# DeltaNet recurrence and MLP mixer in fp32: all four batch elements walk their Grams, joins and recurrence in 64 and 32 wide tiles

## The chip, the cores and the metric

One core of a Trainium2 chip. The kernel is one program for five engines: TensorE (PE, with its weight loads as PEld), VectorE (DVE), ScalarE (ACT), GpSimd (POOL) and SyncE (SP), each of which runs its own instructions in order and waits on semaphores for the others. The metric is the device time of one execution in microseconds (us), lower is better. Everything is fp32.

## The reference

Two parts. The first is a delta rule recurrence, for each of 4 batch elements and 8 heads, over 768 tokens of 48 features:

```python
k_n = k / (np.linalg.norm(k, axis=-1, keepdims=True) + 1e-06)
state = np.zeros((B, H, D, D), dtype=np.float32)
for t in range(S):
    kt, vt, bt = (k_n[:, :, t], v[:, :, t], beta[:, :, t, None])
    y[:, :, t] = np.einsum('bhd,bhde->bhe', q[:, :, t], state)
    v_old = np.einsum('bhde,bhd->bhe', state, kt)
    state = state + bt[:, :, :, None] * np.einsum('bhd,bhe->bhde', kt, vt - v_old)
```

The second takes y as x of shape (4, 768, 384), the heads side by side, and mixes it over tokens and then over channels:

```python
xt = x.transpose(0, 2, 1)
h = np.maximum(xt @ w_tok1, 0.0) @ w_tok2
u = x + h.transpose(0, 2, 1)
h2 = np.maximum(u @ w_ch1, 0.0) @ w_ch2
return (u + h2).astype(np.float32)
```

The weights arrive as float64 and are turned into fp32 on the chip.

## The kernel before

A **unit** u is 128 tokens of one batch element, 24 in all, six to an element. It has two **chunks** of 64 tokens (cc = 0, 1). A **step** t is one chunk of the recurrence, 48 in all, twelve to an element. The 8 heads are taken as 4 pairs p, so a unit has 8 blocks nb = 2p + cc, each for a pair of heads. With a head's 64 rows on half of the 128 partitions, a pair fills them.

The work is split into jobs, Python generators that issue a few instructions between two `yield`s. One letter and one number name a job: `k` loads k and q, `v` loads v, `p` prepares a unit, `i` inverts the triangular blocks of a round of units, `h`, `f` and `j` join the inverted blocks, `r` is a step of the recurrence, `m` is the mixer of an element, `w` turns a piece of weights into fp32. Three more, `x`, `y` and `z`, only multiply zeros on PE and write a PSUM tile that nobody reads. A long string, `order`, written out by hand, says which job moves on next, word by word, and so sets the order of the instructions on every engine. Nothing else schedules.

What a unit goes through:

- `prep` (`p`): k and q are transposed on PE (p_t), ACT copies them to kqt, with features on partitions and tokens along the free side. Then the Gram p_g, k times [k|q], is made for every block, and DVE multiplies it by the mask and by beta into gm. In the first element (u < NCH = 6) it is made per head, with 64 wide weights, one head on each half (line 387). In the other three, ACT first copies k into kbd, a tile of 128x128 blocks with one head in each diagonal corner and zeros elsewhere (line 360), and one 128 wide matmul makes the block of a pair (line 385).
- `invert` (`i`): DVE inverts 32x32 triangular blocks for a whole round of units at once, 14 or 30 pairs of instructions (lines 507 and 512). From the second element on, the blocks pass through DRAM (n_dram, w_dram).
- `join` (`j`): two 32x32 inverses are joined into one of 64x64 by two products p_z and p_x. The first element uses 32 wide tiles (lines 575 and 584), the others zero-padded tiles t11 and zst that make each product 65 columns wide over all 128 partitions (lines 604 and 613).
- `recur` (`r`): for a chunk, r = k·state - v, w = W·r with W the joined inverse, state and y from w. `recur_early` does the first element per head: p_k, p_y, p_w, p_s, and p_y again, 64 wide, head 0 from rows 0 to 63 to rows 0 to 63 and head 1 from rows 64 to 127 to rows 64 to 127. `recur` does the others on pairs: s_bd, r_bd and w_bd hold the two heads' tiles in two corners of a 128x96 block and zeros elsewhere. p_q (line 719) is k·state and q·state in one matmul for a pair, p_w (735) and p_s (743) follow. DVE writes r_bd in two halves (722), ACT copies the q half of p_q into the mixer's input xb (726) and w_bd in two halves (738), DVE updates s_bd (751) and adds the rest of y to xb (759).

`mixer` (`m`) is the same for all elements: p (line 772), p_h (785), then for six chunks of 128 tokens p_ut, p_c with a relu on ACT (811, 819) and p_o (827), which DVE adds to xb (833) and a DMA writes out. The steps of a later element stand between pieces of the mixer of the one before: m0 among units 6 to 17 or so, m1 and m2 after it, and m3 alone at the end.

PSUM has four kinds of buffer: prep (2), seq (2), mlp (3) and warm (1, for the zeros).

## Time and profile before

| | |
|---|---|
| median of 3 runs | 786.44 us (786.2 to 787.96) |
| the profiled execution's own time | 786.3 us |
| span of its trace, first to last instruction | 784.5 us |
| PE busy | 742.1 us, 95% of the span |
| DVE busy | 383.0 us, 49% |
| ACT busy | 256.0 us, 33% |
| POOL busy | 99.5 us, 13% |
| mean granted TensorE clock | 0.952 |

Times below are us from the start of the span. An fp32 matmul stands in the trace as two passes, each with its own weight load, so a count of passes is twice that of the matmuls. Passes overlap in the records: a pass of 128 columns is listed with some 0.28 us though the next may start 0.11 us after it. How long a group takes is therefore read from its start to the start of the next one. A busy share of 95% says that PE always had something in flight, not that it worked at its peak. The granted clock (PEclk) is 1 at full speed and 0.5 when it is halved.

### The profile page before, as it was taken

The page shows a single profiled execution, that of the slowest core. Times are in us where ns is not written, and L with a number is a line of the kernel's source. Part 1 is how long each engine was busy: PE and PEld are TensorE (multiplying, and loading weights), DVE is VectorE, ACT ScalarE, POOL GpSimd, SP SyncE. Part 2 cuts the span into 40 slices and gives each one's busy share as a digit, 9 for nine tenths or more (in the row PEclk, how much of TensorE's full clock was granted, in tenths as well). Part 3 has the DMA queues.
Part 4 walks back from the last instruction along what each step waited for, and adds up shares of the span by engine and source line. Part 5 has one row for each costly group of instructions (what it writes and reads, how often), then busy time and mean ns, then how long its engine had stood idle before and what let it go on. Part 6 is the DMA issues. An engine that isn't in the chain of part 4 may idle for free.

```text
span 784.5 us, 16847 instructions
## 1 busy us (share of the span) xinstructions
PE 742.1 (95%) x6950; PEld 607.9 (77%) x6950; DVE 383.0 (49%) x983; ACT 256.0 (33%) x589; POOL 99.5 (13%) x122
## 2 busy tenths in 40 slices
PE   8879987988899999997899999999999999999998
PEld 6558886657789789776588888778888978688776
DVE  6987778898735724337433538231228433200000
ACT  4546566427543113322124431233121322111110
POOL 2121234314320001110001010010000000000000
PEclk9976568799999999999799999999999999999999
DMA  7834345436524033232032231300011120000000
GB/s 152 170 84 98 84 104 136 92 99 152 132 55 103 14 84 64 36 72 44 13 79 42 47 64 24 83 21 12 21 29 23 35 42 1 11 11 11 11 11 21
DMA packets 151101, 46.82 MB, mean 60 GB/s; under 512 B 142416, under 2 KB 145488, under 8 KB 151024
## 3 DMA queue, kind: packets, MB, share of 16 engines
q1 hardware_dynamic: 151024, 45.74, 26.6%
q8 instruction: 55, 0.90, 0.5%
q14 instruction: 22, 0.18, 0.1%
HBM read 36.27 MB, written 9.44 MB: 58 GB/s over the span
## 4 chain that ended last, share of the span: by engine, by line
PE 79%; DVE 11%; SPq 3%; issue 2%; ACT 2%; DMA 2%; POOL 1%; POOLq 0%; ACTq 0%; DVEq 0%
PE p_o L827 24%; PE p_c L811 23%; PE p_g L385 4%; PE p_s L743 3%; PE p_q L719 3%; PE p L772 3%; DVE x L512 3%; PE p_w L735 3%; DVE sub L507 2%; SPq L292 2%; PE p_h L785 2%; PE p_z L604 2%; PE p_x L613 2%; PE p_t L353 1%; PE p_w L665 1%
## 5 line engine op out<-in xcount | busy, mean ns | idle before, releaser
L827 PE MATMUL p_o<-wc,r 128*128 128x384 f32 x576 | 199.2, 493 | 9.0 <-ACT r L819 8.3
L811 PE MATMUL p_c<-u_t,wc 128*128 128x128 f32 x1728 | 206.5, 276 | 0.6 <-ACT u_t L799 0.6
L811 PEld LDWEIGHTS p_c<-u_t,wc 128*128 128x128 f32 x1728 | 200.0, 192 | 5.1 <-ACT u_t L799 0.8
L827 PEld LDWEIGHTS p_o<-wc,r 128*128 128x128 f32 x576 | 106.3, 192 | 72.2 <-ACT r L819 8.5
L819 ACT ACTIVATE r<-p_c 128x512 f32<-128x512 f32 x72 | 42.9, 597 | 202.1 <-PE p_c L811 201.7
L833 DVE TENSOR_TENSOR xb<-xb,p_o 128x384 f32<-128x384 f32 x24 | 13.3, 554 | 152.6 <-PE p_o L827 152.6
L507 DVE TENSOR_TENSOR sub<-x 128x84 f32<-128x84 f32 (+24 forms) x178 | 61.7, 347 | 10.8 <-DMA x<-n_dram 6.0
L512 DVE TENSOR_TENSOR x<-x,sub 128x84 f32<-128x84 f32 (+24 forms) x178 | 63.3, 356 | 6.1
L364 POOL TENSOR_TENSOR mb<-mask_c,cs 128x512 f32<-128x512 f32 x20 | 21.6, 1079 | 253.2 <-DVE cs L343 217.0
L390 DVE TENSOR_TENSOR gm<-p_g,mb 128x512 f32<-128x512 f32 x48 | 32.7, 685 | 37.1 <-PE p_g L385 31.9
L751 DVE TENSOR_TENSOR s_bd<-s_bd,p_s 48x192 f32<-48x192 f32 x60 | 21.4, 357 | 56.5 <-PE p_s L743 55.3
L230 POOL TENSOR_TENSOR w_f<-w_f,d 128x384 uint32<-128x384 uint32 (+1 forms) x34 | 33.8, 996 | 112.8 <-DVE w_f L223 59.6
L726 ACT COPY xb<-p_q 64x384 f32<-64x384 f32 x33 | 15.7, 475 | 98.9 <-DVE r_bd L722 96.8
L385 PE MATMUL p_g<-kqt,kbd 128*128 128x128 f32 x288 | 41.4, 294 | 1.8 <-ACT kqt L373 0.7
L385 PEld LDWEIGHTS p_g<-kqt,kbd 128*128 128x128 f32 x288 | 38.0, 205 | 6.3 <-ACT kqt L373 1.8
L302 POOL TENSOR_TENSOR v_st<-v_st,nrm 128x384 f32<-128x384 f32 x24 | 20.2, 845 | 177.7 <-DMA v_st<-in_v_dram 167.5
L722 DVE TENSOR_TENSOR r_bd<-p_q,v_st 64x192 f32<-64x192 f32 x66 | 23.1, 350 | 32.9 <-PE p_q L719 18.5
L719 PEld LDWEIGHTS p_q<-s_bd,kqt 128*128 128x128 f32 x264 | 32.9, 192 | 5.3 <-issue 2.4
L772 PE MATMUL p<-xb,w 128*128 128x384 f32 x96 | 34.4, 491 | 1.8 <-DVE w L232 1.8
L719 PE MATMUL p_q<-s_bd,kqt 128*128 128x96 f32 x264 | 34.6, 274 | 1.1 <-DVE s_bd L751 1.1
L785 PE MATMUL p_h<-r,w 128*128 128x384 f32 x96 | 33.7, 492 | 2.0 <-DVE xb L789 1.9
L743 PEld LDWEIGHTS p_s<-w_bd,gm 128*112 128x112 f32 x288 | 32.1, 178 | 3.6 <-ACT w_bd L738 0.6
(122 smaller groups left out, 907.4 us busy)
## 6 DMA issues: line engine op xcount, KB each, us to landing
d<-in_moe_w_ch_dram SPq DMA_DIRECT2D x24, 384.0 KB, 3.4
kpad<-in_k_dram SPq DMA_DIRECT2D x24, 192.0 KB, 3.7
kst<-in_k_dram SPq DMA_DIRECT2D x96, 48.0 KB, 2.7
qpad<-in_q_dram SPq DMA_DIRECT2D x24, 192.0 KB, 3.6
v_st<-in_v_dram SPq DMA_DIRECT2D x96, 48.0 KB, 2.4
out_dram<-xb SPq DMA_DIRECT2D x24, 192.0 KB, 1.9
n_dram<-gm SPq DMA_DIRECT2D x72, 32.0 KB, 1.7
gm<-w_dram SPq DMA_DIRECT2D x72, 32.0 KB, 2.1
```

What stands on the lines that cost most here:

```text
L230: nc.gpsimd.tensor_tensor(out=f, in0=f, in1=lo, op=ALU.add)
L385: nc.tensor.matmul(p_g[:, i], kbd[:, nb], kqt[:, nb])
L390: nc.vector.tensor_tensor(out=gm[:, r, 0 : 2 * C].rearrange("s b (two n) -> s b two n", two=2), in0=p_g, in1=mb.rearrange("s p c t -> s (p ...
L507: nc.vector.tensor_tensor(out=tmp, in0=y[:, :, 0:s, s : s + 1].to_broadcast([n, k, s, w]), in1=y[:, :, s : s + 1, s + 1 : m].to_broadcast( ...
L512: nc.vector.tensor_tensor(out=y[:, :, 0:s, s + 1 : m], in0=y[:, :, 0:s, s + 1 : m], in1=tmp, op=ALU.add,)
L719: nc.tensor.matmul(p_q[:, p], kqt[:, 2 * p + cc], s0[:, p])
L743: nc.tensor.matmul(p_s[0 : C + D, p], gm[:, 2 * p + cc, C:], w_bd[:, p])
L772: nc.tensor.matmul(p_1[dh], piece_of(w1, c, 0)[:, dh * 128 : (dh + 1) * 128], xb[:, c], start=(c == 0), stop=(c == NCH - 1),)
L785: nc.tensor.matmul(p_h, piece_of(w2, j, c * 128)[:, c * 128 : (c + 1) * 128], r1[j], start=(j == 0), stop=(j == NDH - 1),)
L811: nc.tensor.matmul(p_c[:, i], piece_of(wc1, cb, f * 128)[:, f * 128 : (f + 1) * 128], u_t[:, cb], start=(cb == 0), stop=(cb == NCB - 1),)
L819: nc.scalar.activation(r, p_c, ACTF.Relu)
L827: nc.tensor.matmul(p_o, r2[f // FG][:, f % FG], piece_of(wc2, f, 0), start=(f == 0), stop=(f == NHT - 1),)
```

## The change

All four elements now go the way of the first one, per head, in 64 wide and 32 wide tiles:

- kbd, the zero-padded t11 and zst, and the block-diagonal r_bd, w_bd and s_bd are gone, with the copies and clears that they needed. `recur_early` becomes `recur`, and the two branches of `prep` and `join` become one.
- In odd chunks the two heads change places where tokens are on partitions: beta, k and v are loaded with `PAR[par ^ cc]`. A product from features to tokens of head i then goes from rows of half i to rows of half i ^ cc.
- In a Gram, p_g of chunk 0 uses the tiles (rows low, columns low) and (high, high), that of chunk 1 (low, high) and (high, low). The four are issued one after the other, for each pair, into two PSUM buffers. Both buffers are now taken at once.
- In a step, p_k and the first part of p_y are issued together, pair by pair: p_k goes to half i ^ cc and p_y to the other half, so that again four tiles are used in turn. p_s and the second part of p_y are issued together in the same way. p_y collects both parts in PSUM (in the buffer of the zeros from the second element on), and ACT writes it to xb in two halves at the end of the step. DVE's addition to xb and ACT's copy from p_q are gone.
- p_w, p_z and p_x keep two tiles side by side.
- The order string is new up to about step 15, with more words x, y and z (x 15 to 40, y 16 to 62, z 12 to 22). After that it is the old one, with one more word for each step and fewer for `prep`. A y is now half as long: 128 columns instead of 256.

PE's order at step 21 (second element; unit 10 in kqt_104 before and kqt_103 after). Before:

```order
L743 MATMUL p_s<-w_bd,gm 112x96 x4
L811 MATMUL p_c<-u_t,wc_130 128x128 x3
L385 MATMUL p_g<-kqt_103,kbd 128x128 x8
L811 MATMUL p_c<-u_t,wc_130 128x128 x6
L719 MATMUL p_q<-s_bd_117,kqt_104 128x96 x4
L811 MATMUL p_c<-u_t,wc_130 128x128 x6
L735 MATMUL p_w<-r_bd,gm 65x96 x4
```

And now (line 696 is the mixer's p_c, 603 and 604 are p_k and p_y, which go on alternating up to eight of each):

```order
L629 MATMUL p_s<-w_st_114,gm 48x48
L630 MATMUL p_yb<-w_st_114,gm 64x48
L696 MATMUL p_c<-u_t,wc_129 128x128 x3
L376 MATMUL p_g<-kqt_102 64x128 x16
L696 MATMUL p_c<-u_t,wc_129 128x128 x6
L603 MATMUL p_k<-s_st_117,kqt_103 64x48
L604 MATMUL p_yb<-s_st_117,kqt_103 64x48
```

The pieces of the mixer between the groups are the same; each group has two or four times as many matmuls as before.

ACT's order at step 26 (third element, unit 13), around the copy from p_q. Before:

```order
L327 ACTIVATE ksq<-kst 128x384
L799 COPY u_t<-p_ut 128x384
L819 ACTIVATE r_4243<-p_c 128x512
L619 COPY gm<-p_x 32x8x32 x2
L726 COPY xb<-p_q 64x384
L819 ACTIVATE r_4299<-p_c 128x512
L819 ACTIVATE r_4314<-p_c 128x512
L799 COPY u_t<-p_ut 128x384
```

And now (704 is the relu, 684 the copy of u_t, 576 that of p_x):

```order
L322 ACTIVATE ksq<-kst 128x384
L684 COPY u_t<-p_ut 128x384
L704 ACTIVATE r_5005<-p_c 128x512
L576 COPY gm<-p_x 32x8x32 x2
L704 ACTIVATE r_5059<-p_c 128x512
L704 ACTIVATE r_5074<-p_c 128x512
L684 COPY u_t<-p_ut 128x384
```

Nothing that belongs to step 26 stands between the relus any more.

PE's order in the first element, from step 0's p_s to step 1's p_w. Before:

```order
L675 MATMUL p_s<-w_bd,gm 48x48 x8
L688 MATMUL p_y<-w_bd,gm 64x48 x8
L552 MATMUL p_x<-gm,xb 16x16 x32
L575 MATMUL p_z<-t_112,gm 32x32 x16
L646 MATMUL p_k<-s_bd_117,kqt_100 64x48 x8
L656 MATMUL p_y<-s_bd_117,kqt_100 64x48 x8
L665 MATMUL p_w<-r_bd,gm 64x48 x8
```

And now, from the last pair of step 0 to the first of step 1 (line 376 is a Gram of unit 5, line 168 a word y, of four matmuls with zeros):

```order
L629 MATMUL p_s<-w_st_114,gm 48x48
L630 MATMUL p_y<-w_st_114,gm 64x48
L376 MATMUL p_g<-kqt_104 64x128 x16
L168 MATMUL p_warm_132<-warm 64x128
L168 MATMUL p_warm<-warm 64x128 x2
L168 MATMUL p_warm_132<-warm 64x128
L603 MATMUL p_k<-s_st_117,kqt_99 64x48
L604 MATMUL p_y<-s_st_117,kqt_99 64x48
```

A word y has come in ahead of step 1, and three more stand between its p_y and its p_w, where PE went from one straight to the other.

The core of the diff:

```diff
@@ warm_tiles
-                        (p_warm_2 if i == k else p_warm)[out_r, 0:2], warm[r, 0:C],
-                        warm[r, None, 0:128].to_broadcast([C, 2, 128]),
+                        (p_warm_2 if i == k else p_warm)[out_r, 0], warm[r, 0:C],
+                        warm[r, 0:128],
@@ stacked
-                    out=dst[C * par : C * par + C, :, cc], in_=rows[par, cc]
+                    out=dst[PAR[par ^ cc], :, cc], in_=rows[par, cc]
@@ prep
         nc.scalar.copy(kqt_k, p_t)
-        for par in range(2 if u >= NCH else 0):
-            nc.scalar.copy(bd[PAR[par], :, :, C * par : C * par + C], p_t[PAR[par]])
...
-                if u >= NCH:
-                    nc.tensor.matmul(p_g[:, i], kbd[:, nb], kqt[:, nb])
-                for r in PAR if u < NCH else ():
-                    nc.tensor.matmul(p_g[r, i], kqt[r, nb, 0], kqt[r, nb])
...
+        p_g = [ps_prep([128, NP, 2, C], "p_g") for cc in range(2)]
+        for p in range(NP):
+            for cc in range(2):
+                for i in range(2):
+                    nc.tensor.matmul(
+                        p_g[cc][PAR[i ^ cc], p], kqt[PAR[i], 2 * p + cc, 0],
+                        kqt[PAR[i], 2 * p + cc],
+                    )
@@ join, units 6 to 23
-            nc.tensor.matmul(p_z[0 : C + 1, nb], gm_of(u)[:, nb, 0 : C + 1], t11[:, nb])
+            for r, r2 in halves:
+                nc.tensor.matmul(p_z[r2, nb], wt[r, nb, HB:C], t11[r, nb])
...
+                nc.tensor.matmul(p_x[r, nb], zst[r2, nb], wt[r2, nb, HB:C])
@@ recur
-                nc.tensor.matmul(p_q[:, p], kqt[:, 2 * p + cc], s0[:, p])
...
-            nc.scalar.copy(y, p_q[hi].rearrange("s p n -> s (p n)"))
...
+        if b == 0:
+            p_y = ps_mlp([128, NP, D], "p_y")
+        else:
+            p_y = psum.tile([128, NP, D], FP32, name="p_yb", tag="warm", bufs=1)
...
+            for p, i in by_head:
+                f = FEATS[i]
+                nc.tensor.matmul(p_k[PAR[i ^ cc], p], kqt[f, 2 * p + cc, 0], s0[f, p])
+                nc.tensor.matmul(
+                    p_y[PAR[1 - (i ^ cc)], p], kqt[f, 2 * p + cc, 1], s0[f, p],
+                    start=(p == 0), stop=False,
+                )
+            yield
+            nc.vector.tensor_tensor(out=r_st, in0=p_k, in1=v_st[:, :, cc], op=ALU.subtract)
...
+        nc.scalar.copy(w, p_w)
...
+            r = PAR[i ^ cc]
+            if not last:
+                nc.tensor.matmul(p_s[FEATS[i], p], gm[r, 2 * p + cc, 2 * C :], w[r, p])
+            nc.tensor.matmul(
+                p_y[PAR[1 - (i ^ cc)], p], gm[r, 2 * p + cc, C : 2 * C], w[r, p],
+                start=(c == 0 and p == 0), stop=(p == NP - 1),
+            )
...
-        p_y = p_s[lo].rearrange("s p n -> s (p n)")
-        if c > 0:
-            nc.vector.tensor_tensor(out=y, in0=y, in1=p_y, op=ALU.add)
...
+        for i in range(2):
+            nc.scalar.mul(
+                y[:, :, D * i : D * i + D], p_y[PAR[1 - (i ^ cc)]], 1.0 if c else -1.0
+            )
@@ jobs
-        jobs[f"r{t}"] = recur(t) if t >= NQ else recur_early(t)
+        jobs[f"r{t}"] = recur(t)
```

336 lines of the change are left out of this document (105 added, 231 removed).

## The prediction

> **What bounds the kernel now.** I read the span and then a view that cuts it into stretches. The columns are the stretch, its length, the busy time and instructions of PE, PEld, DVE, ACT and POOL, the granted clock, and the DMA share and rate.
>
> ```profile
> span 784.5 us, 16847 instructions
> 0.00:216.20 216.20, 187.38 (x3054) 151.22 (x3055) 177.80 (x438) 115.67 (x269) 63.19 (x78) 0.85 0.53 119
> 50.00:100.00 50.00, 45.09 (x1116) 40.35 (x1116) 38.92 (x101) 30.41 (x76) 14.16 (x15) 0.66 0.43 93
> 100.00:150.00 50.00, 44.13 (x940) 38.63 (x941) 41.90 (x101) 29.13 (x72) 16.23 (x18) 0.73 0.51 114
> 216.20:668.40 452.20, 443.01 (x3248) 370.42 (x3247) 197.47 (x532) 125.40 (x292) 36.35 (x44) 0.99 0.21 43
> 668.40:784.50 116.10, 111.72 (x651) 86.27 (x649) 7.75 (x14) 14.92 (x29) 0.00 (x0) 1.00 0.04 13
> ```
>
> There are three stages. From 216 to 668 us PE is busy for 443.01 of 452.20 us and DVE for less than half: PE bounds, and nearly all that it lacks is one stop, below. From 668 us m3 runs alone, which the change does not touch. Up to 216 us DVE has 177.80 us of work and PE 187.38, at a clock that is halved for long (0.66 and 0.73 between 50 and 150 us): two engines that wait for each other, DVE the nearer to being full in work that must be done, since part of PE's is zeros.
>
> **The middle stage: what goes.** The groups of that stretch, with passes after the x:
>
> ```profile
> L719 PE MATMUL p_q<-s_bd,kqt 128*128 128x96 f32 x232 | 30.2, 273 | 0.0
> L743 PE MATMUL p_s<-w_bd,gm 128*112 128x96 f32 x248 | 29.6, 262 | 0.0
> L735 PE MATMUL p_w<-r_bd,gm 128*65 128x96 f32 x248 | 25.6, 246 | 0.0
> L385 PE MATMUL p_g<-kqt,kbd 128*128 128x128 f32 x192 | 25.2, 277 | 0.7 <-ACT kqt L373 0.7
> L604 PE MATMUL p_z<-t,gm 128*65 128x64 f32 x224 | 15.6, 223 | 0.0
> L613 PE MATMUL p_x<-gm,zst 128*65 128x32 f32 x224 | 15.2, 222 | 0.2 <-ACT zst L608 0.2
> ```
>
> At 8 passes a step and 16 a unit that is 29 p_q, 31 p_s, 31 p_w, 12 p_g, 14 p_z, 14 p_x. Their pace, from start to next start in PE's timeline:
>
> ```profile
> 239.54 1.03 PE L719 MATMUL p_q<-s_bd,kqt 128*128 128x96 f32 x8
> 240.41 1.53 PE L811 MATMUL p_c<-u_t,wc 128*128 128x128 f32 x12
> ...
> 252.14 0.81 PE L827 MATMUL p_o<-wc,r 128*128 128x384 f32 x2
> 252.78 1.95 PE L385 MATMUL p_g<-kqt,kbd 128*128 128x128 f32 x16
> 254.57 0.82 PE L735 MATMUL p_w<-r_bd,gm 128*65 128x96 f32 x8
> 255.23 0.52 PE L827 MATMUL p_o<-wc,r 128*128 128x384 f32 x1
> ...
> 303.18 1.08 PE L613 MATMUL p_x<-gm,zst 128*65 128x32 f32 x16
> 304.10 1.14 PE L604 MATMUL p_z<-t,gm 128*65 128x64 f32 x16
> 305.08 0.88 PE L735 MATMUL p_w<-r_bd,gm 128*65 128x96 f32 x8
> ```
>
> So p_q takes 0.87, p_g 1.79, p_w 0.66, p_x 0.92, p_z 0.98. For p_s I take 0.78: its busy time of a group is 29.6/31 = 0.95, and p_q's record (30.2/29 = 1.04) is 0.17 longer than its pace. Sum: 29 x 0.87 + 31 x 0.78 + 31 x 0.66 + 12 x 1.79 + 14 x 0.92 + 14 x 0.98 = 25.2 + 24.2 + 20.5 + 21.5 + 12.9 + 13.7 = **118 us go**.
>
> **What comes in their place.** The first element already runs such tiles:
>
> ```profile
> 41.64 0.66 PE L174 MATMUL p_warm<-warm 64*64 64x256 f32 x8
> 42.23 1.12 PE L164 MATMUL p_warm<-warm 128*128 128x512 f32 x2
> ...
> 65.48 0.65 PE L575 MATMUL p_z<-t,gm 32*32 32x32 f32 x30
> 66.06 0.67 PE L646 MATMUL p_k<-s_bd,kqt 48*64 48x48 f32 x16
> 66.56 0.52 PE L656 MATMUL p_y<-s_bd,kqt 48*64 48x48 f32 x12
> ...
> 131.49 0.72 PE L552 MATMUL p_x<-gm,xb 32*16 32x16 f32 x64
> 132.14 0.71 PE L646 MATMUL p_k<-s_bd,kqt 48*64 48x48 f32 x16
> ```
>
> Sixteen passes of p_k on two tiles take 0.50 (66.06 to 66.56). Whether four tiles run side by side decides most. Line 174 walks the same four tiles in the same turn, with two PSUM buffers, as p_k and p_y now do: 8 passes of 256 columns in 0.59. One after the other they would need 8 x 0.21 = 1.7, at 0.32 for 384 columns (252.14 to 252.78, two passes). So four run at once, and the 32 passes of a p_k with its p_y, or of p_s with its p_y, take as long as 16 on two tiles: 0.50. A p_w, 16 passes on two tiles, is 0.50 too. Thirty passes of p_z take 0.58, so a p_z or p_x 0.62. For p_g the 128 columns set the pace, eight rounds of four at 0.11 (four transposes of 128 columns in 0.43, next fence), and 0.06 to fill: 0.93.
>
> Each time PE goes from full width to tiles and back it loses something:
>
> ```profile
> 19.38 0.60 PE L353 MATMUL p_t<-ident,kpad 128*128 128x128 f32 x4
> 19.81 0.60 PE L371 MATMUL p_t<-ident,qpad 128*128 128x128 f32 x4
> 20.34 0.66 PE L174 MATMUL p_warm<-warm 64*64 64x256 f32 x8
> ```
>
> Four transposes ahead of transposes take 0.43, ahead of tiles 0.53: 0.10 for going in. The 0.59 of line 174 is two rounds of 0.21 and 0.17 of filling and going out. I take 0.20 for both ways. In the new order PE goes into tiles 97 times in this stage. Sum: 91 x 0.50 + 28 x 0.62 + 12 x 0.93 + 97 x 0.20 = 45.5 + 17.4 + 11.2 + 19.4 = **94 us come**. PE gains **24 us**, step by step about 0.2, and most from p_g. The bounds: with half the price of a switch and no fill, 39; with twice that price, 5.
>
> A page of the Trainium skill, TensorEngine Tiling (Array Packing), section Performance Considerations (Instruction Overhead), speaks against small tiles: each matmul has about 60 cycles of overhead, so a short one costs as much as one of 60 columns. With TensorE's 2.4 GHz from the Trainium skill's page Trainium Architecture — The Big Picture (The five engines, in one table), an estimate by these pages is 0.025 us for each pass, 0.80 for 32 passes, and 60 x 0.30 + 28 x 0.18 = 23 us more than my sum. The trace does not agree: 64 passes start in 0.65 us (131.49 to 132.14), 0.010 each.
>
> **The stop.** Nearly all of PE's idle time in this stage has one cause (ACT, DVE and PE timelines):
>
> ```profile
> 374.36 0.72 DVE L722 TENSOR_TENSOR r_bd<-p_q,v_st 64x192 f32<-64x192 f32 x2
> ...
> 375.12 0.48 ACT L726 COPY xb<-p_q 64x384 f32<-64x384 f32 x1 [11.55 <-DVE r_bd L722]
> 375.62 1.09 ACT L819 ACTIVATE r<-p_c 128x512 f32<-128x512 f32 x2
> ...
> 376.27 10.56 PE L827 MATMUL p_o<-wc,r 128*128 128x384 f32 x24 [8.26 <-ACT r L819]
> ```
>
> ACT's copy of y out of p_q is held until DVE has read the same p_q for r_bd, and DVE is deep in an inversion. Behind the copy on ACT stand two relus that have long had their input, and behind them PE's p_o. PE idles 8.26 us and then runs 24 passes in 10.56 instead of 24 x 0.32 = 7.7, since the clock has dropped. The change removes the copy: y's part stays in PSUM, and no ACT instruction of this step stands ahead of the relus. What is late next is p_w, which needs r_st from DVE, but in the order that stands behind two dozen further pieces of the mixer, and the inversion itself goes on waiting for PE's p_o as before, only earlier. I take the whole of it: 8.3 + 2.8 = **11 us**. The lower bound is nothing.
>
> New waits: p_y has one PSUM bank, so a step's first p_y waits for ACT's two writes of y of the step before, and all of PE's work queues behind it.
>
> ```profile
> L696 ACT ACTIVATE xb<-p_y 64x192 f32<-64x192 f32 x24 | 7.8, 325 | 8.4 <-PE p_y L688 8.1
> ```
>
> Two of these, 0.65, stand beside two writes of the state of 0.35 each on DVE, which p_k must wait for anyway. Where a relu is ahead on ACT it costs some 0.5. I put down **3 us** for this; none to 15 (0.5 on each of 29 steps) are its bounds. In return r_st and w are written by one instruction instead of two, so both waits inside a step shorten by about 0.3.
>
> **The first stage.** DVE loses these, of the first 215 us:
>
> ```profile
> L722 DVE TENSOR_TENSOR r_bd<-p_q,v_st 64x192 f32<-64x192 f32 x6 | 2.1, 349 | 0.1
> L597 DVE STREAM_TRANSPOSE t<-gm 32x256 f32<-32x256 f32 x8 | 3.4, 431 | 0.5 <-DMA gm<-w_dram 0.4
> L759 DVE TENSOR_TENSOR xb<-xb,p_s 64x384 f32<-64x384 f32 x3 | 1.6, 549 | 0.1
> ```
>
> Half of the first two and all of the third: 4.4 us. PE saves about 0.5 on each p_k with p_y and p_s with p_y of the first element, and 0.86 on its six p_g (sixteen rounds of two passes at 0.11 become eight of four): some 16 us at full clock. The added zeros cost: 62 y of 0.42 (two rounds of 0.11 and a switch) for 16 of 0.59, 25 x of 0.22, 10 z of 0.86: 31 us of PE. They buy clock: between 50 and 150 us, at 0.66 and 0.73, PE was at half speed for some 61 us and lost 30 by it. So PE's load is about even, and what can shrink is DVE's idle time there, 100 - 38.9 - 41.9 = 19.2 us. I take a third of it, 6.4. With the 4.4: **11 us**. Bounds: 23 gained, if all of it goes; 11 lost, if the clock stays low (31 - 16 - 4.4).
>
> **Sum.** 784.5 - 24 - 11 + 3 - 11 = 741.5 us of span. The profiled run took 786.3 for 784.5, and the median of the runs is 786.4, so 1.8 are added: **743 us**.
>
> **Rivals.** (1) *The stop stays or moves* (another wait takes its place when PE runs ahead of DVE's inversions): 743 + 11 = 754. For it: DVE's inversions keep their length. Against: DVE is busy for 197 of 452 us. (2) *The first stage doesn't shorten*, as zeros stand in the way of steps: 754, and 765 if it loses 11. For it: a y now stands in most gaps. Against: half the PE clock there is lost today. (3) *Four tiles run as two* for real operands: each p_k with p_y and p_s with p_y takes 0.47 more, p_g 0.87: 28 + 10 = 38 us, 781. Line 174 speaks against it, but with zeros and one moving operand. (4) *Slower: the array empties at each change of width.* The same page of the Trainium skill, section Tiling Modes, says that changing the mode drains TensorE. In the trace's terms, each change would expose a whole record, 0.28 (a pass of p_g) to 0.52 (the p_o pass at 255.23), 0.8 for both ways instead of 0.20, and another 0.3 to refill: 97 x 0.9 = 87, 830 us. It decides from 0.65 for both ways, where 97 x 0.45 eats the 43 gained. Against it: 0.10 and 0.17, measured above.
>
> Chances: forecast 0.60, (1) 0.14, (2) 0.16, (3) 0.04, (4) 0.04, and 0.02 for no effect at all. The range, 724 to 768, takes in more from the first stage and the cheap switch at its low end, and (1) and (2) at its high end. A measurement here can tell about 0.2% from no change; beyond that, faster 0.93, within it 0.02, slower 0.05.
>
> **What would show it.** Right: p_k with p_y from start to next start in 0.5 to 0.7 at full clock, p_g in about 1.1, no stop of PE at the third element's first inversion (here at 368 us), m0's first chunk done near 205 us, clock above 0.85 from 50 to 150 us, the last 116 us unchanged. Wrong: rounds of two in the timeline, PE idle for p_k behind ACT's y, or DVE waiting longer in the first stage.

## The result: 765.7 us, and where the time went

| | before | after |
|---|---|---|
| median | 787.2 us beside the change | 765.7 us (762.9 to 768.7) |
| ratio to before | | 0.9725, 95% interval 0.9673 to 0.9777 |
| profiled execution, span | 786.3, 784.5 us | 763.25, 761.5 us |
| start to the end of m0's first chunk | 216.7 | 201.3 |
| from there to the end of m2's last chunk | 457.9 | 450.1 |
| the rest, m3 | 109.9 | 110.1 |

The change is faster by 2.7%, 21.5 us. The forecast was 43. Times here and below are medians, and ratios leave out one execution of 1598 us, of e7, that stands apart from all others. The stages are cut at the ends of DVE's additions of p_o to xb, which close a chunk. First the view that cuts the span into stretches, for the changed kernel, with the two windows that the prediction used (columns as there: stretch, length, busy time and instructions of PE, PEld, DVE, ACT and POOL, granted clock, DMA share and rate).

```profile
span 761.5 us, 23082 instructions
0.00:201.30 201.30, 180.21 (x3945) 133.43 (x3946) 162.47 (x430) 108.38 (x257) 58.53 (x69) 0.92 0.58 128
201.30:651.40 450.10, 438.37 (x5586) 338.80 (x5586) 162.44 (x459) 109.14 (x270) 35.05 (x40) 0.99 0.22 44
651.40:761.50 110.10, 105.61 (x621) 82.08 (x619) 6.70 (x13) 14.05 (x26) 0.00 (x0) 1.00 0.04 13
50.00:100.00 50.00, 44.61 (x1376) 36.41 (x1370) 38.70 (x113) 30.55 (x77) 13.16 (x15) 0.81 0.41 89
100.00:150.00 50.00, 44.30 (x1051) 32.44 (x1052) 40.36 (x105) 24.71 (x62) 15.48 (x16) 0.93 0.58 129
```

The same cut of the kernel before:

```profile
0.00:216.70 216.70, 187.88 (x3059) 151.72 (x3060) 178.30 (x439) 115.67 (x269) 63.19 (x78) 0.85 0.53 119
216.70:674.60 457.90, 448.71 (x3275) 374.20 (x3274) 198.07 (x534) 126.26 (x294) 36.35 (x44) 0.99 0.20 43
```

The first stage gained 15.4 us, the middle 7.8, m3 nothing. The middle held the stop, for which 11 were forecast. So beside the stop the middle did not gain its 24 less 3; it lost some 3. That is more than the missing 22; the first stage gave 4 back.

The stop itself is gone. PE's timeline of the change at the place, from p_w of step 26 on:

```profile
368.22 0.67 PE L617 MATMUL p_w<-r_st,gm 64*64 64x48 f32 x16
368.82 0.55 PE L680 MATMUL p_ut<-ident,xb 128*128 128x128 f32 x3
369.20 1.46 PE L712 MATMUL p_o<-wc,r 128*128 128x384 f32 x4
370.58 1.10 PE L376 MATMUL p_g<-kqt 64*64 64x128 f32 x32
```

p_o follows p_ut at once, with no idle time.

**What the groups cost now.** Sums over all groups of the middle, each from its start to the start of the next group on PE (before 216.2 to 668.4, after 201.3 to 645.2), in us:

| | before | after |
|---|---|---|
| p_q, now p_k with p_y | 25.5 | 22.4 |
| p_s, now p_s with p_y | 24.6 | 24.2 |
| p_w | 21.0 | 19.8 |
| p_g | 22.2 | 12.8 |
| p_z and p_x | 26.6 | 18.2 |
| these together | 119.9 | 97.4 |
| p_c | 134.4 | 145.6 |
| p_o, p, p_h, p_t | 180.5 | 192.1 |
| p_ut, before with the stop of 8.3 | 13.7 | 5.6 |

The changed groups gave 22.5 back. The mixer's groups and the transposes, which nobody changed, took all of it. Why, stands in the rows. A p_k with p_y, the p_c behind it and the next p_w, after the change:

```profile
223.47 0.25 PE L603 MATMUL p_k<-s_st,kqt 48*64 48x48 f32 x1
...
224.09 1.60 PE L696 MATMUL p_c<-u_t,wc 128*128 128x128 f32 x12
225.62 0.67 PE L617 MATMUL p_w<-r_st,gm 64*64 64x48 f32 x16
```

and the p_w behind the same p_c before, which began at 240.41 there (a row of the prediction):

```profile
241.78 0.82 PE L735 MATMUL p_w<-r_bd,gm 128*65 128x96 f32 x8
```

Twelve passes of p_c took 1.37 from start to start, and take 1.53 now. Pass by pass, over the 96 excursions into tiles of this stage, the trace shows three parts: the last full-width pass ahead of tiles holds the next one up for 0.098 longer (9.4 us), the first full-width pass starts 0.15 after the last tile pass, where tile passes follow each other in 0.02 (12.5 us), and the second full-width pass starts 0.103 late (9.8 us). That is **0.33 for an excursion**, counted on top of tile passes at their own pace, as the forecast's sum counts them, and not 0.20. The third part was not in the sum at all, and the parts on the full-width side are booked under p_c, p_o and the mixer's other groups.

**Two by two.** A p_s with p_y of step 24, and one of step 25:

```profile
334.13 0.24 PE L629 MATMUL p_s<-w_st,gm 64*48 64x48 f32 x1
...
334.75 1.56 PE L670 MATMUL p_h<-r,w 128*128 128x384 f32 x4
...
339.56 0.30 PE L629 MATMUL p_s<-w_st,gm 64*48 64x48 f32 x4
339.68 0.29 PE L630 MATMUL p_yb<-w_st,gm 64*64 64x48 f32 x4
...
340.55 1.56 PE L670 MATMUL p_h<-r,w 128*128 128x384 f32 x4
```

0.62 from the first row to p_h in the even chunk, 0.99 in the odd one, and so in every step. The code says why: p_s goes from rows of half i ^ cc to half i, p_y from rows of half i ^ cc to half 1 - (i ^ cc). With cc = 1 the latter is i as well: both use the same tile, and only two of the four work. "In the same way", as the change is described above, holds for the issue, not for the tiles, in odd chunks.

**New waits.** PE's idle time of the middle was 9.2 us before, 8.3 of it the stop; it is 11.7 now, in eleven places, and behind three of them the granted clock is 0.50 for 3.4 us (from 390.3, 496.1 and 588.2). Four of the longest, of PE's timeline:

```profile
303.91 0.66 PE L363 MATMUL p_t<-ident,qpad 128*128 128x128 f32 x4 [1.73 <-ACT gm L576]
...
389.92 0.25 PE L604 MATMUL p_yb<-s_st,kqt 48*64 48x48 f32 x1 [1.18 <-ACT xb L644]
...
495.18 0.69 PE L573 MATMUL p_x<-gm,zst 32*32 32x32 f32 x32 [1.75 <-issue]
...
587.77 0.76 PE L564 MATMUL p_z<-t,gm 32*32 32x32 f32 x32 [1.79 <-DVE t L559]
```

The third names no releaser; DVE's timeline does:

```profile
493.46 0.55 DVE L674 TENSOR_TENSOR xb<-xb,p_h 128x384 f32<-128x384 f32 x1 [3.70 <-PE p_h L670]
493.93 0.55 DVE L325 TENSOR_REDUCE ksum<-ksq 128x8 f32<-128x384 f32 x1
494.39 0.68 DVE L382 TENSOR_TENSOR gm<-p_g,mb 128x512 f32<-128x512 f32 x1
```

A Gram now takes both prep buffers at once. The p_x wants one of them, and DVE empties the first only behind an addition to xb that waits for p_h.

**The first stage.** DVE's idle time there did not change: 216.7 - 178.3 = 38.4 before, 201.3 - 162.5 = 38.8 after. Its work fell by 15.8. DVE's costliest groups of the stage (busy time, mean ns of one), before:

```profile
L512 DVE TENSOR_TENSOR x<-x,sub 128x108 f32<-128x108 f32 (+20 forms) x58 | 22.0, 379 | 2.0
L223 DVE SCALAR_TENSOR_TENSOR w_f<-d,w_f 128x384 uint32<-128x384 uint32 (+1 forms) x34 | 21.6, 634 | 0.7
L507 DVE TENSOR_TENSOR sub<-x 128x108 f32<-128x108 f32 (+20 forms) x58 | 20.5, 353 | 1.1
```

and after:

```profile
L218 DVE SCALAR_TENSOR_TENSOR w_f<-d,w_f 128x384 uint32<-128x384 uint32 (+1 forms) x34 | 18.6, 550 | 0.6
L503 DVE TENSOR_TENSOR x<-x,sub 128x108 f32<-128x108 f32 (+20 forms) x58 | 17.2, 296 | 2.0
L498 DVE TENSOR_TENSOR sub<-x 128x108 f32<-128x108 f32 (+20 forms) x58 | 16.7, 287 | 1.3
```

The same 116 instructions of the inversions take 8.6 us less, and the same 34 of w_f take 3.0 less. What made them long before stands in the timelines of DVE and POOL:

```profile
87.19 0.98 DVE L507 TENSOR_TENSOR sub<-x 128x112 f32<-128x112 f32 x1
88.21 0.79 DVE L512 TENSOR_TENSOR x<-x,sub 128x112 f32<-128x112 f32 x1
...
87.04 1.00 POOL L230 TENSOR_TENSOR w_f<-w_f,d 128x384 uint32<-128x384 uint32 x1 [5.97 <-DVE w_f L223]
88.00 0.86 POOL L375 TENSOR_TENSOR gm<-kst,cs 128x384 f32<-128x384 f32 x1
```

This size takes 0.27 by itself. Beside GpSimd's work it ends 0.13 us after that has ended. Before, 20 of the 116 ran for more than half of their time beside GpSimd, 0.76 each, the other 96 0.28; after, 2 did. With the new order of issue the two hardly meet; no run takes that order back alone.

### The profile page after: what moved, and what is told of

Same layout as the page of the kernel before. It is cut to its first block, busy times and chain, and to the rows that moved or that the text cites. A ratio compares the mean times of both kernels' runs of the same rounds, so it can differ in the third digit from the quotient of the medians.

```text
span 761.5 us, 23082 instructions
## 1 busy us (share of the span) xinstructions
PE 724.2 (95%) x10148; PEld 554.3 (73%) x10148; DVE 331.6 (44%) x899; ACT 231.6 (30%) x553; POOL 93.6 (12%) x109
## 4 chain that ended last, share of the span: by engine, by line
PE 79%; DVE 10%; issue 3%; ACT 3%; SPq 3%; DMA 1%; POOL 0%; ACTq 0%; DVEq 0%; POOLq 0%
PE p_c L696 26%; PE p_o L712 24%; PE p_h L670 3%; PE p_w L617 3%; PE p L657 3%; DVE sub L498 3%; DVE x L503 3%; PE p_g L376 3%; PE p_s L629 2%; PE p_k L603 2%; PE p_z L564 2%; PE p_yb L630 2%; PE p_x L573 2%; SPq L287 2%; PE p_t L348 1%
## 5 line engine op out<-in xcount | busy, mean ns | idle before, releaser
L696 PE MATMUL p_c<-u_t,wc 128*128 128x128 f32 x1728 | 211.8, 280 | 1.2 <-DVE xb L674 0.6
L639 DVE TENSOR_TENSOR s_st<-s_st,p_s 48x192 f32<-48x192 f32 x80 | 28.0, 350 | 88.6 <-PE p_yb L630 75.0
L158 PE MATMUL p_warm<-warm 128*128 128x128 f32 (+1 forms) x124 | 40.6, 437 | 1.1 <-DVE warm L106 1.1
L603 PEld LDWEIGHTS p_k<-s_st,kqt 48*64 48x64 f32 x704 | 27.7, 138 | 14.7 <-issue 8.7
L621 ACT COPY w_st<-p_w 128x192 f32<-128x192 f32 x48 | 15.4, 320 | 75.3 <-PE p_w L617 75.1
L629 PE MATMUL p_s<-w_st,gm 64*48 64x48 f32 x704 | 34.1, 215 | 4.1 <-ACT w_st L621 4.1
L644 ACT ACTIVATE xb<-p_yb 64x192 f32<-64x192 f32 x72 | 23.4, 325 | 47.1 <-PE p_yb L630 46.3
L603 PE MATMUL p_k<-s_st,kqt 48*64 48x48 f32 x704 | 33.9, 227 | 2.7 <-issue 1.9
L617 PEld LDWEIGHTS p_w<-r_st,gm 64*64 64x64 f32 x704 | 26.4, 142 | 13.7 <-issue 6.3
L629 PEld LDWEIGHTS p_s<-w_st,gm 64*48 64x48 f32 x704 | 28.3, 124 | 11.0 <-ACT w_st L621 4.8
```

The lines of the kernel that those rows point to most:

```text
L158: nc.tensor.matmul(p_warm[:, 0:m], zero, zero[:, None, :].to_broadcast([128, m, 128]))
L603: nc.tensor.matmul(p_k[PAR[i ^ cc], p], kqt[f, 2 * p + cc, 0], s0[f, p])
L617: nc.tensor.matmul(p_w[PAR[i], p], gm[PAR[i], 2 * p + cc, 0:C], rest[PAR[i], p])
L629: nc.tensor.matmul(p_s[FEATS[i], p], gm[r, 2 * p + cc, 2 * C :], w[r, p])
L696: nc.tensor.matmul(p_c[:, i], piece_of(wc1, cb, f * 128)[:, f * 128 : (f + 1) * 128], u_t[:, cb], start=(cb == 0), stop=(cb == NCB - 1),)
```

## The experiments

The middle is the better yardstick for what happens in it: kernels that differ from the change only in the first stage (e7, e11, e12) walked it in 450.0 to 450.1 us. It is no exact one: e5 and e6, whose middle has the same instructions too, took 448.3 and 454.1. The granted clock was 0.50 there for two stretches of 3.4 us in e5, for 20.5 us in all in e6, and for 10.2 in the change. So a difference of a few us between two middles means little by itself.

The first stage scatters more: in the change and the kernels with the same instructions up to there (e5, e6, e8, e10; e3 nearly so) its end fell between 197.7 and 205.0, and a kernel's time carries that scatter. It too goes with the clock. The ends of the five, in order, are 197.7, 201.3, 201.3, 203.6 and 205.0, at a mean granted clock of 0.95, 0.92, 0.92, 0.90 and 0.89. The first and the last of them, e5 and e10:

```profile
0.00:197.65 197.65, 178.98 (x3945) 131.91 (x3946) 162.64 (x430) 108.19 (x257) 58.52 (x69) 0.95 0.58 130
0.00:204.97 204.97, 186.21 (x3945) 138.45 (x3946) 162.28 (x430) 108.46 (x257) 58.52 (x69) 0.89 0.56 126
```

DVE's work is the same to 0.4 us. Why the clock differs between executions of the same instructions, no run shows.

**e1: the recurrence of elements 2 to 4 at full width.** Everything else stays as in the change.

```diff
-        jobs[f"r{t}"] = recur(t)
+        jobs[f"r{t}"] = recur(t) if t < NQ else recur_pairs(t)
@@ recur_pairs, as recur before, with positions j and heads j ^ cc
+                nc.tensor.matmul(p_q[:, p], kqt[:, 2 * p + cc], s0[:, p])
...
+                    out=r_bd[PAR[j], :, ends[j]], in0=p_q[lo, :, ends[j ^ cc]],
...
+            nc.scalar.copy(y, p_q[hi])
+        for r, e in zip(PAR, ends):
+            nc.scalar.copy(w_bd[r, :, e], p_w[lo, :, e] if c > 0 else p_w[r])
```

> The changed kernel, but elements 2 to 4 walk the recurrence as before, a pair of heads in one full-width matmul (p_q, p_w, p_s with zero-padded s_bd, r_bd, w_bd); Grams and joins stay in tiles, heads stay swapped in odd chunks, the first element and the order of issue stay. y's first part is copied out of p_q just ahead of the two copies of w, not at once. PE's excursions into tiles from step 16 on fall from 98 to 40. Theory A (an excursion costs 0.33, not 0.20, and p_s with p_y in odd chunks walks two tiles instead of four): tiles cost the recurrence 66.4 us in groups and 58 x 0.20 = 11.7 on their neighbours, 78 in all, and full width 71 as before: 7 us faster than the change, 759 (753 to 764). Theory B (the prices of the prediction hold, and waits ate the gain): 91 x 0.50 + 58 x 0.20 = 57 against 71, so 13 us slower than the change, about 779.

Measured: 766.0 us, ratio to before 0.973 (0.9691 to 0.9769), the middle 451.4 (the change: 450.1).

```profile
206.50:657.90 451.40, 440.31 (x3930) 355.94 (x3929) 191.04 (x534) 114.17 (x270) 35.01 (x40) 0.98 0.21 44
```

Neither theory: full width is not 7 us better and not 13 worse. The recurrence's groups took 75.5 us (p_q 27.5, p_w 22.3, p_s 25.7) instead of 66.4, and the mixer's groups and transposes 332.9 instead of 343.3. So what the tiles of the recurrence save in their own groups they lose at their borders. PE's idle time was 11.1, much of it at the same joins and transposes as in the change.

**e2: no swap of heads.**

```diff
-                    out=dst[PAR[par ^ cc], :, cc], in_=rows[par, cc]
+                    out=dst[PAR[par], :, cc], in_=rows[par, cc]
@@ the same in load_beta, prep and recur
-                nc.tensor.matmul(p_k[PAR[i ^ cc], p], kqt[f, 2 * p + cc, 0], s0[f, p])
+                nc.tensor.matmul(p_k[PAR[i], p], kqt[f, 2 * p + cc, 0], s0[f, p])
```

> The changed kernel without the swap of heads in odd chunks: each head keeps its half of the rows everywhere. Theory A (in odd chunks p_s and the second part of p_y use the same tile of the four, so 32 passes go two by two): p_s with p_y falls from 0.99 to 0.61 in odd chunks, as in even ones, 9 us less over 24 steps; p_g, now on two tiles, goes from 0.98 to about 1.85, 16 us more over 18 units; 766 + 7 = 772 (767 to 776), less if the first element hides its share. Theory B (the 0.99 has another cause, such as the writes into two PSUM banks or the wait for w): p_s with p_y stays at 0.99 in odd chunks, and the time is about 780.

Measured: 776.3 us, 0.9867 (0.9842 to 0.9891). All p_s with p_y now take 0.61, in odd chunks too; their sum in the middle fell from 24.2 to 19.5, and that of p_g rose from 12.8 to 22.4. The middle took 456.5, 6.4 longer, near the 4.9 of these two. So the odd chunks' 0.99 is the shared tile (20 steps have it, not 24: the last step of an element has no p_s). The swap is still right: it costs the steps 5 us and saves the Grams 10. The time is 0.3 above theory A's range, with a first stage of 207.8.

**e3: one after the other.**

```diff
                 nc.tensor.matmul(p_k[PAR[i ^ cc], p], kqt[f, 2 * p + cc, 0], s0[f, p])
+            for p, i in by_head:
+                f = FEATS[i]
                 nc.tensor.matmul(
                     p_y[PAR[1 - (i ^ cc)], p], kqt[f, 2 * p + cc, 1], s0[f, p],
@@ and so for p_s and the second part of p_y
```

> The changed kernel with p_k and the first part of p_y issued one after the other (eight and eight matmuls) instead of in turns, and p_s and the second part of p_y too. If four tiles run side by side only when they are issued in turns: p_k with p_y goes from 0.61 to 0.99 in every step, p_s with p_y in even chunks too, and in odd chunks p_s with p_y stays at 0.99, since it walks two tiles in either order. That is 45 x 0.38 = 17 us more in the middle and up to 6 in the first element: 783 to 789. If TensorE ran four tiles no better than two, nothing changes: 766.

Measured: 771.5 us, 0.9785 (0.9718 to 0.9852); the middle 458.1, 8.0 longer. p_k with p_y went from 0.61 to 0.88, p_s with p_y to 0.83 in even chunks, and stayed at 0.96 in odd ones:

```profile
342.02 0.56 PE L631 MATMUL p_s<-w_st,gm 64*48 64x48 f32 x16
342.41 0.63 PE L634 MATMUL p_yb<-w_st,gm 64*64 64x48 f32 x16
342.97 0.59 PE L674 MATMUL p_h<-r,w 128*128 128x384 f32 x1
```

So four tiles do run side by side, and issuing them in turns is worth 0.21 to 0.27 a group; for the odd chunks the order hardly matters. It is less than the 0.38 expected, probably since the last of the first eight and the first of the second eight still overlap where they use different tiles; no run separates that. With less than was expected in the groups, the time came out 12 us below the range put down.

**e4: the kernel before, with y copied later.**

```diff
-            nc.scalar.copy(y, p_q[hi].rearrange("s p n -> s (p n)"))
@@ one yield later
+        if c > 0:
+            nc.scalar.copy(y, p_q[hi].rearrange("s p n -> s (p n)"))
         for r, e in zip(PAR, ends):
             nc.scalar.copy(w_bd[r, :, e], p_w[lo, :, e])
```

> The kernel before, with one line moved: ACT's copy of y out of p_q stands ahead of the two copies of w, one word of the order later, instead of behind DVE's r_bd. Theory A (the stop of 8.3 us at 368 us and the 2.8 of slow clock behind it come from this copy standing ahead of two relus): 787 - 11 = 776, with no stop there. Theory B (the stop only moves, since DVE stays late with r_bd): 787, with a stop of several us at another wait of the third element.

Measured: 777.3 us, 0.9874 (0.9855 to 0.9893).

```profile
216.50:664.60 448.10, 446.19 (x3274) 373.14 (x3273) 197.90 (x533) 126.66 (x294) 36.28 (x44) 1.00 0.21 44
```

The middle lost 9.8 of its 457.9 us, PE is idle for 1.9 in it, and no new stop appears. The stop was that one copy, worth 10 us. It follows that the middle of the kernel before, without its stop, is 2 us shorter than that of the change.

**e5 and e6: what an excursion costs.** In m3, where nothing else runs, a matmul with zeros is put between the second and the third of a p_c block, in a 64 wide tile (e5) or at full width (e6). Each ran once, and the chunks of m3 are read from its trace.

```diff
@@ mixer, within a p_c block (e5; e6 has all rows and 128 weights)
+                        if b == 3 and i < 2 and cb == 1:
+                            nc.tensor.matmul(
+                                p_c[PAR[0], i, 0:48], warm[PAR[0], 0:C], warm[PAR[0], 0:48],
+                                start=False, stop=False,
+                            )
```

> The changed kernel with 36 more excursions into tiles in m3, which runs alone: in the first two of each four p_c blocks one matmul with zeros, 64 x 64 weights and 48 columns, is added into the running sum, between the second and the third of its three matmuls. Read from the 16.1 us that lie between the ends of two chunks of m3, six excursions each. Theory A (the switch as it reads in the trace of the change: 0.10 going in, 0.12 coming out, 0.10 more on the first full-width pass, with some 0.06 for the two passes): 16.1 + 6 x 0.39 = 18.4 a chunk, 14 us in all. Theory B (0.20 for both ways, as predicted): 16.1 + 6 x 0.26 = 17.7, 9 us in all.

> Its control: the same 36 matmuls with zeros in m3, with 128 x 128 weights over all rows, so without a change of width. Two passes of 48 columns at 0.06 (a pass of 32 columns took 0.058 at full width in the kernel before): 16.1 + 6 x 0.12 = 16.8 a chunk, under 5 us in all, by both theories; a pass that is held by its weight load would take 0.11, and a chunk 17.4. The difference to the tile variant is what the change of width costs.

Measured: a chunk of m3 takes 18.7 in e5, 17.45 in e6, 16.1 in the change: 0.437 and 0.223 for each insertion. PE's timeline of e5:

```profile
699.81 0.94 PE L696 MATMUL p_c<-u_t,wc 128*128 128x128 f32 x7
700.69 0.31 PE L702 MATMUL p_c<-warm 64*64 64x48 f32 x2
700.93 0.94 PE L696 MATMUL p_c<-u_t,wc 128*128 128x128 f32 x6
701.79 0.31 PE L702 MATMUL p_c<-warm 64*64 64x48 f32 x2
```

Pass by pass the 0.437 is, each time alike to a nanosecond or two: 0.093 more ahead of the tile, 0.094 from its first pass to its second (one tile, so nothing runs beside it), 0.148 to the first full-width pass, and 0.101 more to the second. So the three parts that the change showed among other work (0.098, 0.15, 0.103) are here too, where nothing else runs, and the chunk of 18.7 is near theory A's 18.4, not B's 17.7. The page TensorEngine Tiling (Array Packing) of the Trainium skill, section Tiling Modes, says that a change of mode drains TensorE; the trace agrees that each costs something.

The size depends on what it is set against. The control was dearer than expected: two 48 column passes between passes of 128 take as long as two of 128. By the measure put down before the run, tile less control, the change of width costs 0.21. Set against tile passes at the pace that they have among other tiles, as in the forecast's sum and in the 0.33 above, it costs more, since a full-width pass in the place of a tile's is itself not cheap. Either way it is far below rival (4)'s 0.9.

**e7: as few zeros as before.**

```diff
-    w3 w1*2 b x w1*3 y k0 y k0*4 z w3*2 y x k0 w3 k1*3 y k1*3 k2*2 p0*2 y k2 p0 k2 y x b
+    w3 w1*2 b w1*3 k0*5 w3*2 k0 w3 k1*3 y k1*3 k2*2 p0*2 k2 p0 k2 x b k2*2 w3 b p0*3 w2
@@ x 40 to 15, y 62 to 16, z 22 to 12, evenly over the string
```

> The changed kernel with as many words of zeros as before, evenly thinned: x 40 to 15, y 62 to 16, z 22 to 12; nothing else moves. Theory A (the zeros buy clock, and the clock buys a part of the 15 us of the first stage): the granted clock from 50 to 150 us falls from 0.87 to 0.7 or below, m0's first chunk ends at 207 to 216 instead of 201 to 206, and the whole at 770 to 780. Theory B (DVE sets the pace there, and PE's clock doesn't matter): the clock falls, and the end stays at 763 to 769.

Measured: 766.0 us, 0.9718 (0.9656 to 0.9779). Its windows:

```profile
50.00:100.00 50.00, 42.44 (x1261) 35.52 (x1254) 38.02 (x113) 30.05 (x76) 11.99 (x13) 0.67 0.39 87
100.00:150.00 50.00, 41.69 (x899) 31.79 (x898) 38.05 (x98) 24.58 (x61) 15.94 (x17) 0.69 0.57 130
```

The clock is back at 0.67 and 0.69, and the time did not change, as theory B had it. So the zeros buy clock, and the two together come out even. That is not to say that the clock is worth nothing: the zeros that went were PE's work (it is busy for 169.0 us up to the end of the first stage at 204.3, for 180.2 in the change), and where the instructions are the same, the stage ended earlier at the higher clock.

**e8: eight words of the order moved.** Three of the pieces:

```diff
-r17*2 m0 r17 p14*2 p13 m0 p13*3 r17 r18*2
+r17*2 m0 r17*2 p14*2 p13 m0 p13*3 r18*2
-p22 m2 p23 p22 j18*2
+p22*2 m2 p23 j18*2
-r40 i6*3 m2 j20 j21 j20
+r40 j21 i6*3 m2 j20*2
```

> The changed kernel with eight words of the order moved, so that what PE waits for in the middle stage comes earlier or has work in front of it: the writes of y of steps 17, 23 and 27 ahead of a relu or a copy, ACT's copy of p_x of unit 11 ahead of a square root, DVE's first gm of unit 22 ahead of an addition to xb, DVE's transposes of unit 21 ahead of three pairs of the inversion, and two pieces of p_o in front of the wait of a p_z and of a p_s. Theory A (part of the missing gain is lost in waits that the shorter groups laid bare and in the slow clock behind them, 11.7 and some 4 us): 7 to 11 us less than the change, 755 to 759. Theory B (PE would be late in any case, a wait that goes comes back at the next place): 763 to 766.

Measured: 752.3 us, 0.9569 (0.9528 to 0.9609).

```profile
201.30:640.60 439.30, 434.56 (x5586) 336.20 (x5586) 162.46 (x459) 109.04 (x270) 35.09 (x40) 1.00 0.22 45
```

The middle is 10.8 us shorter than in the change with the same instructions: 7.0 of PE's idle time are gone (11.7 to 4.7), and PE's busy time fell by 3.8, with the clock at 0.50 in one stretch of 3.4 us instead of three. The waits did not come back. The kernel before had no such waits to lose: beside its stop PE was idle for 1.9 us (e4). So half of the missing gain was lost in the old order, which lays waits bare when the groups get shorter.

**e9: full width again, without the waits.**

```diff
@@ e1, with e8's order, and
-            p_q = ps_seq([128, NP, 2 * D], "p_q")
+            p_q = psum.tile([128, NP, 2 * D], FP32, name="p_q", tag="warm", bufs=1)
@@ the copy of y moves from ahead of w's copies to the step's last word
```

> The kernel of e1 (elements 2 to 4 recur in full-width pairs, Grams and joins in tiles) with the eight moved words of e8, p_q in the bank of the zeros, and its copy of y at the end of the step. With the waits gone from both, it shows what the tiles of the recurrence are worth by themselves, against e8 (752.3). Theory A (prices of groups and switches as measured): full width 25.5 + 24.8 + 20.7 = 71.0 us, tiles 64 in groups and 58 x 0.20 = 12 on their neighbours, 76: full width is 5 us faster, 747. Theory C (the two are worth the same, as e1 and the change were): 750 to 755. Theory B (tiles at the predicted prices, 57): full width is 14 us slower, 766.

Measured: 761.4 us, 0.9661 (0.9634 to 0.9689), the middle 441.0.

```profile
210.20:651.20 441.00, 433.95 (x3930) 350.56 (x3930) 191.78 (x535) 113.63 (x270) 35.00 (x40) 1.00 0.22 45
```

In the middle PE is busy for 434.0, in e8 for 434.6: there theory C holds, and the tiles of the recurrence are worth next to nothing either way (e8 has one stretch of 3.4 us at clock 0.50 in it, e9 none, which is worth 1 to 2 us). The whole is 9 us slower than e8 and misses theory C's range, because the first stage, which holds steps 12 to 15, ends at 210.2 here (and at 206.5 in e1). The granted clock is lower there, 0.89 and 0.90 against 0.92 in e8; whether that is all of it, no run separates.

**e10: fewer excursions.** Two of the pieces, against e8:

```diff
-p13*2 m0*2 p13 r17 m0 k15 m0 r17*2
+m0*2 p13*2 r17 m0 k15 m0 r17 p13 r17
-p22*2 m2 p23 j18*2 m2*2 r36
+m2 p23 m2*2 p22*2 r36
```

(the two words j18 of the second piece now follow p_s of step 35.)

> The kernel of e8 with nineteen more words moved: ten tile groups of Grams and joins that stood alone among full-width work now stand beside a group of a step, so PE goes into tiles 89 times instead of 99, with the same matmuls; and the write of y of step 21 and DVE's r_st of step 40 come earlier, where e8 still waits 0.9 and 1.1 us. Theory A (a switch costs 0.33, a change between 64 and 32 wide tiles 0.12): 10 x 0.33 - 7 x 0.12 = 2.5 and 2 of waits, 748. Theory B (0.20 a switch, and waits come back elsewhere): 751 to 753.

Measured: 749.7 us, 0.9504 (0.9473 to 0.9534), the fastest of all.

```profile
205.00:639.20 434.20, 430.87 (x5586) 334.58 (x5585) 162.24 (x458) 109.14 (x270) 35.04 (x40) 1.00 0.22 46
```

The middle is 5.1 us shorter than in e8, 3.7 of it PE's busy time with the same passes, 1.4 its idle time. Up to 1.7 of the 3.7 is clock, since e8's stretch at 0.50 is gone as well. The other 2.0 lie nearer to theory A's 2.5 than to 10 x 0.20 - 7 x 0.12 = 1.2 at theory B's price, and the waits did not come back elsewhere; but this run alone doesn't fix the price. The median fell by 2.6, to a place between the two theories; the two profiled executions differ by 1.4 only, since this one's first stage ended at 205.0 and e8's at 201.3, which is the scatter named above.

**e11 and e12: GpSimd beside the inversions.** e11 adds 14 instructions that read nothing of DVE's, e12 lets them read the product just made.

```diff
@@ invert, in every second pair of the first two rounds (e12)
+            if early and s % 2:
+                few = tmp.rearrange("b k s w -> b (k s w)")[:, None, 0:28]
+                nc.gpsimd.tensor_tensor(
+                    out=idle, in0=idle, in1=few.to_broadcast([128, 14, 28]), op=ALU.mult
+                )
```

> The changed kernel with 14 instructions added on GpSimd, each beside every second pair of DVE's first two inversions (a product of a 128x384 tile with itself, about 0.8 us, read by nobody). In the kernel before, 20 of the 116 DVE instructions of the inversions up to 216 us ran beside GpSimd work and took 0.76 us on the average, the other 96 took 0.28; in the change 2 of 116 do. Theory A (the new order took GpSimd's work out of the inversions, and that is the larger part of what the first stage gained): the 14 put it back, 14 or more DVE instructions take 0.8 to 1.1 instead of 0.2 to 0.3, DVE is busy 8 to 10 us longer, m0's first chunk ends 5 to 10 us later than 201 to 206, and the whole takes 771 to 776. Theory B (DVE has room there, its inversions do not set the pace): DVE is busier by as much, and the time stays at 763 to 769.

Measured: 765.7 us, 0.9742 (0.9695 to 0.979). It doesn't decide between the theories, but serves as a control for e12: GpSimd ran ahead, six of the 14 in a row before the first inversion began, and the inversions took 35.2 us instead of 33.8.

> As e11, but each of the 14 added GpSimd instructions (392 columns, about 0.85 us) reads the product that DVE has just written in this pair, so it cannot run ahead as it did in e11 (six of them in a row before the inversion began) and stands beside the next DVE instructions. Theory A (GpSimd's work beside the inversion is what the new order took away, and DVE's work sets the end of the first stage): some 14 DVE instructions take 0.6 to 1.1 instead of 0.2 to 0.3, the inversions 42 to 45 us instead of 33.9, m0's first chunk ends 5 to 10 us later than in the change (201 to 206), the whole takes 771 to 776. Theory B (DVE has room there): the inversions take as much longer, and the time stays at 763 to 769.

Measured: 775.0 us, 0.9848 (0.9819 to 0.9877). DVE and POOL in the first inversion:

```profile
38.02 0.28 DVE L505 TENSOR_TENSOR x<-x,sub 128x112 f32<-128x112 f32 x1
38.33 0.97 DVE L500 TENSOR_TENSOR sub<-x 128x112 f32<-128x112 f32 x1
39.34 0.28 DVE L505 TENSOR_TENSOR x<-x,sub 128x112 f32<-128x112 f32 x1
...
38.07 1.10 POOL L511 TENSOR_TENSOR idle<-idle,sub 128x392 f32<-128x392 f32 x1 [0.89 <-DVE sub L500]
```

and its stages:

```profile
0.00:209.60 209.60, 183.35 (x3945) 135.87 (x3946) 172.91 (x430) 108.48 (x257) 74.57 (x84) 0.90 0.56 123
209.60:659.60 450.00, 438.39 (x5586) 338.50 (x5586) 162.41 (x459) 108.99 (x270) 35.05 (x40) 0.99 0.21 44
```

The inversions took 40.8 us, 7.0 more than in the change; DVE was busy for 10.4 more, the first stage ended 8.3 later, and the middle is the same to 0.1. Theory A: DVE's work bears on the end of the first stage, and GpSimd beside it makes that work longer. In e11 GpSimd had nearly as much work (70.4 us in the first stage, 74.6 here, 58.5 in the change), and nothing was lost. DVE's idle time did not grow in e12 either (36.7 us, 38.8 in the change), so DVE wasn't waiting for GpSimd's results. DVE's work is not all that sets the end, though: e2, whose Grams take longer on PE, ended the stage at 207.8 with 161.0 us of it. The Trainium skill's page SBUF — State Buffer, section SBUF: two separate sides, states the mechanism: the two share a pair of ports as an exclusive lock, taken against GpSimd by a DVE instruction with two SBUF inputs, and whoever comes second is blocked for the whole of the other's instruction. The trace agrees: 0.97 beside, 0.28 by itself, and the end 0.13 us after GpSimd's.

## Where the prediction was right and where it failed

**The stop, 11 us: right.** e4 takes it away alone and gains 9.8 in the middle and 9.4 in the time.

**The first stage, 11 us: the size about right (15.4), the reason mostly wrong, so the size is luck.** It was to come from a third of DVE's idle time and 4.4 of DVE's work. DVE's idle time stayed (38.4 and 38.8), and 15.8 of its work went: the 4.4 were about right (the transposes, r_st and the additions to xb), but 8.6 more went in inversions and 3.0 in w_f that the diff doesn't touch. The argument on the clock that stood behind it, zeros that cost PE 31 us and buy 30, is borne out by e7: with the zeros and their clock gone, the time is the same. It gave no reason for DVE to idle less, and DVE didn't.

**The middle, 24 us: wrong.** This is the step that failed. The groups that go were priced nearly rightly (118 forecast, 119.9 measured), and so was p_g (0.93 without the way out; 0.92 ahead of other tiles, 1.03 ahead of full width). Three prices on the other side failed, and one was too high:

- "I take 0.20 for both ways": it is 0.33 in the change, and e5 shows the same three parts. I had read the entry rightly from the warm tiles (0.10) but guessed the exit as part of 0.17 of filling, and never looked at the pass behind the first full-width one. 96 x 0.13 = 12.5 us.
- "the 32 passes of a p_k with its p_y, or of p_s with its p_y, take as long as 16 on two tiles": true for p_k and for even chunks; in the 13 odd steps of the middle that have a p_s it takes 0.38 more, 4.9 us. The index arithmetic in the diff would have told it.
- "I put down 3 us" for new waits: PE's idle time beside the stop rose by some 10 (1.9 in e4, 11.7 in the change), 7 more than that, and the clock drops behind the waits cost some 4; e8 gets 10.8 of it back by moving eight words. The wait named in the prediction, a step's first p_y behind ACT's two writes of y, is three of the eleven places, 2.8 us; most of the others are at joins and transposes, where a shorter group laid a chain through DVE, ACT or a PSUM buffer bare. Rival (1) had the kind of this (another wait when PE runs ahead), with one place instead of eleven, and a price of 11.
- The tile passes themselves ran in 74.2 us with the odd chunks' 4.9 in them, and in 69 without, against 74 in the sum. 5 us the other way.
- Two smaller terms: the sum had no price for going between 64 and 32 wide tiles, some 25 times at 0.12, 3 us; and the groups that went took 2 more than forecast.

12.5 + 4.9 + 7 + 4 - 5 + 3 - 2 = 24. The middle missed its forecast of 24 - 3 = 21 by 23: it lost 2 against e4. The terms are read from single traces, so an agreement within a few us is all that can be asked. The whole time, 765.7, lies within the range, near its upper end; that end was put there for rivals (1) and (2), so it says little for the sum.

**The rivals.** Four tiles run as two (3): not in p_k with p_y, but in the odd chunks' p_s with p_y, for a reason that (3) did not name. The array empties (4): its threshold was 0.65 for both ways, the price is 0.33, so the kind is right and the size a third of its 0.9. Of what "would show it", p_k with p_y at 0.61, p_g near 1.0, the missing stop, the first chunk at 201, the clock (0.81 and 0.93, 0.87 on the mean) and the unchanged end all came as the forecast had them, and it was still 22 us off: none of these rows lies where the loss was, in the groups beside the changed ones. Of the signs of being wrong, two came as well: PE idle behind ACT's y, and tiles used two at a time in odd chunks.

## What to carry to other kernels

Price a change of tile width by the groups on both sides of it, to the second pass behind: here some 0.33 us each time, so that a group whose passes save less than that gains nothing, unless it stands beside other tiles. When groups get shorter under an order written by hand, look first at what PE waits for afterwards; eight moved words were worth more than half as much as the whole change (13.4 us against 21.5), and with ten groups moved together the time came to 749.7, 0.9504 of before. Before crediting a gain to the engine that was edited, compare the same unedited instructions in both traces: in the first stage they had become shorter.

## What the runs showed of the hardware

- A full-width stretch behind tiles pays twice: 0.15 to its first pass and 0.10 more to its second. In e5 it is 0.148 and 0.101 each time; in the change the first is 0.12 behind 32 wide tiles and 0.20 behind a Gram.
- A 48 column pass at full width between 128 column passes saves nothing: two of them add 0.223 (e6).
- Products on the same tile go one after the other however they are issued: 32 passes took 0.99 on two tiles and 0.61 on four (steps 25 and 24; e2 turns the one into the other).
- DVE's products of two SBUF tiles take up to 1.1 us beside GpSimd instead of 0.2 to 0.4; e12 makes 7 us of that at will.
- PE can be busy for 89% of the time at a granted clock of 0.70 (before, 50 to 150 us). Behind a stop of 1.2 to 1.8 us the clock was 0.50 for 3.4 us in some executions and not in others: in the change behind three of the long stops, in e5 behind two.
- The same instructions ended the first stage between 197.7 and 205.0 us and the middle between 448.3 and 454.1, the later the lower the granted clock. What moves the clock from one execution to the next is not settled.
